# Two passages of a fused attention and two-layer expert kernel: where the order of experts is worked out, when a gather is issued, in how many parts rows are written

## The chip, the cores and the metric

The kernel runs on one core of one Trainium2 chip, as one program. The metric is the device time of an execution in microseconds (us). The core's engines work side by side, each through its own queue in order: PE (matmuls; PEld loads its weights), DVE, ACT, POOL, and SP, which here issues DMAs. Between engines semaphores order the work, so an instruction that waits holds back all that stands behind it on its engine.

## The reference

```python
def reference(**kwargs):
    ...
    attn_out = _attn_ref(**attn_kwargs)         # clustered attention: 2 x 8 heads x 768 x 64
    x = np.ascontiguousarray(attn_out.transpose(0, 2, 1, 3)).reshape(B * S, H * D)
    x = _moe_ref(x=x, **moe_kwargs)             # layer 1
    return _moe2_ref(x=x, **moe2_kwargs)        # layer 2

def _moe_ref(x, w_gate, w1, w2, capacity):      # 1536 tokens, 512 wide, 8 experts, 1024 inside
    ...
    expert_idx = np.argmax(logits, axis=1)      # one expert for each token
    ...
    h = np.maximum(np.einsum('ecd,edf->ecf', disp, w1), 0.0)
    y = np.einsum('ecf,efd->ecd', h, w2)
    ...
            out[i] = gate_w[i] * y[expert_idx[i], pos[i]]
```

Layer 2 is of the same kind, with a second gate (a sigmoid) and no capacity. Which tokens an expert gets is known only once the rows before it are done: layer 1 needs all of attention, layer 2 all of layer 1.

## The kernel before

Attention runs first, pair of heads by pair, and each half of a batch's rows is scaled and written to a table in DRAM, `x1d` (row: 512 values, gate, token number, one-hot). After that come eighteen **units**, nine of layer 1 (0 to 8) and nine of layer 2 (9 to 17). A unit is up to 392 rows of one expert. Experts are taken by size: the layer's largest first, in two units (128 and 64 rows in layer 1, 256 and 136 in layer 2), so that the first can start before all tokens are routed. Unit 7 has 168 rows, unit 8 (the last of layer 1) 120, unit 9 256, unit 10 136.

**A unit's work.** `gather` (POOL, an indirect DMA) fetches its rows, `meta` (POOL) reads their gate and token; `entry` turns 128 rows on PE and splits them into two float16 halves (`xh` on ACT, `xl` on DVE). `mm1` makes the inner values in eight steps f, of twelve matmuls each, into one of three PSUM buffers; ACT writes `hh`, and the rest `hl` comes either from DVE straight out of PSUM, or, for the f that `FP` lists for the unit, from ACT to `hr` and from there on POOL. `hr` has one buffer, so the next `hr` waits until POOL has read it. `mm2` makes the output in four steps d; in unit 9 it works by token (`pz`). `piece` splits half a weight tile as loaded (`raw`) into `wh` (ACT) and `wl` (DVE, one piece late); `PIECES` says before which f or d of a unit one is issued. A weight tile of 1 MB has four `raw` buffers; SP loads the next when a tile's second `wl` is done.

**Between the layers.** `run` goes through the units. Beside the matmuls it advances generators by one `yield` at set places (once before each step, in the first units of a layer where `SA` and `SB` say so); the engines' order is thus the order in which this code is written and its yields fall. `exit1` takes a unit of layer 1 out: it turns its rows back, works out their layer 2 logits (`pq`, `lt`, `lg`), and scales them; `routed` does the routing of a group of units: choice, place of each row in its expert's list, `R.codes` (low and high part of the place), write of the rows to the table `x2d`, `R.invert` (one-hots `av` and `rv` on DVE, whose matmul lists the rows of each expert by place), and `R.select`, which picks one expert's indices once `R.order` (eight to ten small DVE operations) has sorted the experts by count. The last group is units 6, 7 and 8. After group (4, 5), the "cut", layer 2's first two experts are fixed and unit 9's gather gets its indices (`idx2a`), from rows so far alone; after the last group unit 10 and those behind get theirs (`idx2`). Between attention and layer 1 `after_half` does the same with `x1d`: the last half batch is routed while unit 0 (128 rows) runs, and unit 1 is gathered when `idx1` is there.

Places the text speaks of: `after_half`'s `end` branch (L1560 to L1617), `hr` (L952 to L957), `run` (L1104 to L1121), `exit1`'s `rows` (L1688 to L1706), `routed` (L1796 to L1844).

Of the kernel before, what the change touches and what calls it, by code (L numbers as in the profile page):

```python
# [8 lines left out]
F32 = mybir.dt.float32  # L9
# [715 lines left out]
class MoE:  # L725
# [24 lines left out]
    FB = 0  # L750
    FP = {0: (2, 3, 4, 5, 6, 7), 5: (1, 3, 5), 7: (1, 3, 5, 7), 8: (1, 3, 5), 9: (3, 4)}
    FY = 7
    SA = (1, 1, 1, 0, 1, 0, 0, 0, 0, 0, 1, 1)
    SB = (1, 1, 1, 1, 1, 1, 1, 1, 1, 1, 1, 1)
    Q = 2

    def __init__(self, tc, ctx, ident, R, XW, ND, stages, ps_t):
        nc = tc.nc
        self.tc, self.nc, self.ident, self.R, self.XW, self.ND = tc, nc, ident, R, XW, ND
        DT = self.DT = F16  # L760
        self.pool = lambda name, bufs, **k: ctx.enter_context(tc.tile_pool(name=name, bufs=bufs, **k))
        self.ps_t = ps_t
        self.raw = self.pool("m_raw", 4, side="right")
        self.rings = []
        self.units = [u for s in stages for u in s.units]
        self.ranks = [(s, j) for s in stages for j in s.ranks]
        for s, r0 in zip(stages, (0, stages[0].E)):
            for u in s.units:
                u.r = r0 + s.ranks.index(u.j)
        self.most = max(u.rows for u in self.units)  # L770
        self.G = 4 * len(self.ranks)
        self.fl, self.flt, self.okr, self.reg = {}, {}, {}, {}
        self.rawt, self.chunk = {}, {}
        self.tasks, self.lows = [], []
        self.nload = self.nsplit = self.half = 0
        self.credit = 0
        self.ngather = self.nmeta = 0
        self.limit = self.RING - 1

# [155 lines left out]
    def mm1(self, u, f):  # L935
# [16 lines left out]
        if f in self.FP.get(self.units.index(u), ()):  # L952

            hr = self.sm.tile([128, 256], F32, tag="hr", name="hr", bufs=1)
            nc.scalar.activation(hr[:, :N], p[:, :N], AF.Relu)  # L955
            nc.gpsimd.tensor_tensor(hl[:, f, :N], hr[:, :N], hh[:, f, :N], op=ALU.subtract)
            return  # L957
# [117 lines left out]
    def run(self, task):  # L1075
# [3 lines left out]
        for i, u in enumerate(units):  # L1079
# [24 lines left out]
            for d in range(4):  # L1104
# [3 lines left out]
                if d == 3 and u.opens:  # L1108
                    self.need(4 * u.r + 3)
                    self.flags(u.r)  # L1110
                self.mm2(u, d)
                if d % 2 and u.closes:
# [5 lines left out]
            if head:  # L1118
                assert nxt.gt, "unit not gathered"
                for k in range(len(nxt.tiles)):  # L1120
                    self.entry(nxt, k)  # L1121
# [180 lines left out]
def tile_kernel(tc, q, k, v, centroids, wg1, w11, w12, cap_in, wg2, wog2, w21, w22, out,  # L1302
# [15 lines left out]
    with ExitStack() as ctx:  # L1318
# [27 lines left out]
        if True:  # L1346
# [87 lines left out]
            def after_half(b, hf, rows):  # L1434
# [125 lines left out]
                if end:  # L1560
# [5 lines left out]
                    pp = positions()  # L1566
                    turns(places(), gates(), load_order())
                    scale(2)
                    for i in (0, 2, 1):
                        write(nc.sync, slice(i, i + 1))  # L1570
# [17 lines left out]
                while not next(inv):  # L1588
                    if not end:
                        yield  # L1590
                yield
                if not end:
# [55 lines left out]
        def exit1(unit, ys):  # L1648
# [39 lines left out]
            def rows():  # L1688
# [7 lines left out]
                if group is groups[-1]:  # L1696
# [6 lines left out]
                    us = small("us", len(ns))  # L1703
                    nc.vector.scalar_tensor_tensor(us, u, XSUM, sx[:, ks], op0=ALU.mult, op1=ALU.mult)
                    for i, n in enumerate(ns):
                        nc.scalar.mul(xo[i][:n, :DM], ps[i][:n], us[:n, i:i + 1])  # L1706

            if unit is group[-1]:
# [4 lines left out]
        def routed(group, t0, T, rows):  # L1713
# [43 lines left out]
            if not last:  # L1757
                yield from turns_by(K[1], scales())
            for _ in range(1 if last else K[5]):
                yield  # L1760
# [35 lines left out]
            def gates():  # L1796
                yield from gate
                nc.vector.scalar_tensor_tensor(g2, rx, 1.0 / XSUM, g2, op0=ALU.mult, op1=ALU.mult)
                for i, (x, n) in enumerate(xos):
                    nc.gpsimd.tensor_copy(x[:n, DM:DM + 1], g2[:n, i:i + 1])  # L1800

            def write():
                r0 = 1 + group[0].row
                for x, n in xos:
                    nc.sync.dma_start(x2d[r0:r0 + n], x[:n])
                    r0 += n

            if last:
                turns(places(), load_order(), gates())
                write()  # L1810
# [4 lines left out]
            while not next(inv):  # L1815
                if not last and K[4]:
                    yield
            more = first_experts() if cut else iter(())
            for _ in range(KL if last else K[3]):
# [8 lines left out]
            if cut:  # L1828
                while next(more, more) is not more:
                    next(more, None)  # L1830
                    yield
                R.select(M.sm, ro[0], tab2, idx2a, 0, 1)
                s2.reg[:2] = [ro[1][0:1, j:j + 1] for j in range(2)]
                s2.units[0].src = x2d[:1 + group[-1].row + group[-1].rows]
                s2.units[0].idx = idx2a[:, 0]
            if last:
                RO = ro[0]
# [111 lines left out]
```

## Time and profile before

| | us |
|---|---|
| runs, median of 3 | 626.52 (625.83 to 628.45) |
| profiled execution | 623.46 |
| its span, first to last instruction | 621.7 |
| PE busy | 570.0 (92%) |
| DVE busy | 466.4 (75%) |
| ACT busy | 421.8 (68%) |
| POOL busy | 216.4 (35%) |

Times below are us from the start of the span. 1.8 us of the profiled execution lie outside the span. Busy shares are averages over all stages; a stage is read by the wait that ends last in it. An engine's idle time is put down to its releaser, the instruction whose end let it go on.

### The profile page before, as it was taken

The numbers are of one execution on the slowest core, as the hardware profiler recorded it, in microseconds if no ns is written. First come the engines' busy times: TensorE is split into PE (matmuls) and PEld (weight loads), VectorE is DVE, ScalarE is ACT, GpSimd is POOL, SyncE is SP. The second block draws the span as 40 slices with busy tenths as digits, with TensorE's granted clock in tenths as the row PEclk, the third lists the DMA queues.
The fourth block names the chain that finished last, engine by engine and source line by source line (L and its number), as shares of the span: only waits on it lengthen the run. The fifth ranks groups of instructions, "written<-read, shape, count | busy, mean of one in ns | idle before, by whom it ended". The sixth has DMA issues, their size and how long they took to land.

```text
span 621.7 us, 14524 instructions
## 1 busy us (share of the span) xinstructions
PE 570.0 (92%) x5428; PEld 467.1 (75%) x5428; DVE 466.4 (75%) x1185; ACT 421.8 (68%) x902; POOL 216.4 (35%) x427
## 2 busy tenths in 40 slices
PE   7899999998999998986799999997788999999993
PEld 2676767676767675656778998996777888999993
DVE  4776777677989676867577778789678566979881
ACT  3666666777676667963585687776774566979781
POOL 7702020201341110105743355636523723253541
PEclk9999999999999999999899999999999999999997
DMA  5589654656519891522456856976963677898930
GB/s 138 155 208 289 166 135 118 143 134 134 148 29 224 258 249 23 198 69 105 146 179 236 277 181 206 305 259 191 302 206 98 220 222 240 293 307 291 333 126 23
DMA packets 75518, 117.55 MB, mean 189 GB/s; under 512 B 10504, under 2 KB 43400, under 8 KB 75441
## 3 DMA queue, kind: packets, MB, share of 16 engines
q1 hardware_dynamic: 72017, 106.76, 57.4%
q0 software_dynamic: 3264, 9.72, 4.8%
q8 instruction: 45, 0.74, 0.5%
q14 instruction: 32, 0.26, 0.1%
q10 hardware_dynamic: 160, 0.07, 0.0%
HBM read 84.28 MB, written 12.87 MB: 156 GB/s over the span
## 4 chain that ended last, share of the span: by engine, by line
PE 61%; DVE 15%; ACT 11%; issue 4%; DMA 4%; POOL 2%; SPq 0%; ACTq 0%; DVEq 0%; POOLq 0%
PE ph L949 15%; PE py L1021 13%; PE av L280 9%; PE pss L238 8%; PE ppt L268 6%; PE pz L996 3%; DVE nm L246 3%; DVE wl L846 3%; ACT pe L254 2%; PE pyo L1637 2%; ACT wh L839 2%; ACT pt L270 1%; PE pxt L926 1%; PE plog L153 1%; DMA x2d<-xo 1%
## 5 line engine op out<-in xcount | busy, mean ns | idle before, releaser
L846 DVE SCALAR_TENSOR_TENSOR wl<-raw,sw,wh 128x1024 f16<-128x1024 f32 x128 | 163.6, 1285 | 19.0 <-ACT wh L839 18.8
L839 ACT ACTIVATE wh<-raw,sw 128x1024 f16<-128x1024 f32 x128 | 146.1, 1148 | 3.0 <-DMA x<-ot 2.5
L246 DVE TENSOR_REDUCE nm<-pss 128x1 f32<-128x768 f32 x96 | 91.4, 952 | 41.5 <-PE pss L238 37.8
L254 ACT ACTIVATE pe<-pss,nm 128x768 f32<-128x768 f32 x96 | 87.1, 907 | 24.3 <-DVE nm L246 24.3
L949 PEld LDWEIGHTS <-wh 128*128 128x128 f16 x1152 | 87.7, 99 | 17.4 <-issue 12.8
L238 PE MATMUL pss<-y,x 128*128 128x384 f32 x384 | 95.4, 370 | 4.0 <-ACT pe L254 3.2
L268 PE MATMUL ppt<-ident,pe 128*128 128x128 f32 x576 | 80.5, 275 | 3.3 <-ACT pt L270 1.4
L238 PEld LDWEIGHTS pss<-y,x 128*128 128x128 f32 x384 | 64.7, 194 | 24.6 <-issue 12.5
L270 ACT COPY pt<-ppt 128x384 f32<-128x384 f32 x128 | 57.9, 482 | 29.6 <-PE ppt L268 29.3
L949 PE MATMUL ph<-xh,wh 128*128 128x192 f16 (+14 forms) x576 | 67.3, 240 | 9.9 <-ACT hr L955 4.6
L268 PEld LDWEIGHTS ppt<-ident,pe 128*128 128x128 f32 x576 | 69.2, 142 | 8.9 <-ACT pt L270 2.3
L1021 PEld LDWEIGHTS <-wh 128*128 128x128 f16 x960 | 72.4, 99 | 4.3 <-issue 1.0
L280 PE MATMUL av<-pt,v 128*64 128x384 f32 x384 | 68.8, 494 | 0.0
L949 PE MATMUL ph<-xl,wh 128*128 128x192 f16 (+14 forms) x576 | 67.2, 240 | 0.4 <-DVE xl L928 0.3
L949 PE MATMUL ph<-xh,wl 128*128 128x192 f16 (+14 forms) x576 | 67.3, 240 | 0.0
L951 ACT ACTIVATE hh<-ph 128x128 f16<-128x128 f32 (+14 forms) x144 | 44.6, 316 | 25.9 <-PE ph L949 24.7
L958 DVE SCALAR_TENSOR_TENSOR hl<-ph,hh 128x192 f16<-128x192 f32 (+14 forms) x126 | 40.8, 335 | 26.1 <-ACT hh L951 25.9
L1021 PE MATMUL py<-hh,wh 128*128 128x192 f16 (+13 forms) x480 | 46.6, 239 | 1.5 <-ACT hh L951 1.0
L1021 PE MATMUL py<-hl,wh 128*128 128x192 f16 (+13 forms) x480 | 46.8, 239 | 0.5 <-DVE hl L958 0.2
L949 PEld LDWEIGHTS <-wl 128*128 128x128 f16 x576 | 45.5, 99 | 1.9
L280 PEld LDWEIGHTS av<-pt,v 128*64 128x64 f32 x384 | 24.8, 136 | 28.4 <-issue 28.3
L1021 PE MATMUL py<-hh,wl 128*128 128x192 f16 (+13 forms) x480 | 46.1, 239 | 0.0
(326 smaller groups left out, 873.4 us busy)
## 6 DMA issues: line engine op xcount, KB each, us to landing
raw<-in_moe_w SPq DMA_DIRECT2D x64, 1024.0 KB, 6.2
y<-kh SPq DMA_DIRECT2D x31, 192.0 KB, 4.0
x<-qh SPq DMA_DIRECT2D x30, 192.0 KB, 4.2
q<-in_q SPq DMA_DIRECT2D x8, 384.0 KB, 4.9
k<-in_k SPq DMA_DIRECT2D x8, 384.0 KB, 4.6
x<-ql SPq DMA_DIRECT2D x16, 192.0 KB, 3.5
v<-in_v SPq DMA_DIRECT2D x8, 384.0 KB, 3.3
out<-zt SPq DMA_DIRECT2D x1, 3072.0 KB, 11.3
```

Source lines behind the costliest of these rows:

```text
L238: nc.tensor.matmul(p[:, hf, :W], xx[:, c * P:(c + 1) * P], yy[:, hf * W:(hf + 1) * W], start=a, stop=o)
L246: nc.vector.tensor_reduce(nm, p[:, :, :W], axis=AX.XY, op=ALU.max, negate=True)
L254: nc.scalar.activation(pe, p[:, :, :W], AF.Exp, bias=d["nm", c, j], scale=1.0, accum_out=d["sm"][:, c, j:j + 1])
L268: nc.tensor.transpose(p[:, kc * P:(kc + 1) * P], pe[:, kh, kc * P:(kc + 1) * P], ident)
L270: eng(pt[:, kh * HALF:(kh + 1) * HALF, (c % HALF) * P:(c % HALF + 1) * P], p.rearrange("p (a b) -> p a b", a=HALF))
L280: nc.tensor.matmul(p[j * D:(j + 1) * D, :W], d["v"][:, j, kc, :], d["pt", hf, j][:, kc, :], start=(kc == 0), stop=(kc == C - 1))
L839: nc.scalar.activation(hi[:, :, s], x[:, :, s], AF.Copy, scale=sw)
L846: nc.vector.scalar_tensor_tensor(lo[:, :, s], x[:, :, s], sw, hi[:, :, s], op0=ALU.mult, op1=ALU.subtract, accum_out=fl)
L949: nc.tensor.matmul(p[:, :N], w[:, c, fs], x[:, c, :N], start=(k == 0), stop=(k == 11))
L951: nc.scalar.activation(hh[:, f, :N], p[:, :N], AF.Relu)
L958: nc.vector.scalar_tensor_tensor(hl[:, f, :N], p[:, :N], 0.0, hh[:, f, :N], op0=ALU.max, op1=ALU.subtract)
L1021: nc.tensor.matmul(p[:, :N], w[:, f, s], x[:, f, :N], start=(k == 0), stop=(k == 23))
```

## The change

Six edits:

1. `after_half`, `end`: the third row block is scaled (`scale(2)`) ahead of the places instead of after them, and the order of the experts (`load_order`) is worked out behind the inversion's one-hots instead of in turns with the places. `SA` gets a step before d = 1 of unit 0, so that the inversion's matmul stands on PE one d earlier.
2. `mm1`: `hr` is one tile kept for the whole run; units of at most 128 rows use its two halves in turns, by f.
3. `FP`: unit 7 has `hr` and POOL for f = 5, 7 instead of 1, 3, 5, 7; unit 8 for 1, 2, 5, 6 instead of 1, 3, 5.
4. `routed`, cut: indices are selected and the gather of unit 9 is issued as soon as the order is there, instead of after all of `first_experts`, and at once instead of at `run`'s next place for it.
5. `exit1`, `routed`, last group: the 512 values of the rows of units 6 and 7 are written to `x2d` when they are scaled, their last 12 columns (gate, token, one-hot) with unit 8's whole rows at the end, in reverse order of the units; the order of the experts behind the inversion's one-hots, as in 1; one `yield` more before the places, which puts f = 3 of unit 9 ahead of their matmuls on PE.
6. `PIECES` and `run`: a piece goes from d = 3 of unit 8 to f = 1 of unit 9, and unit 10's first 128 rows are turned before d = 3 of unit 9 instead of after it.

```diff
-              (0, 1, 0, 1, 1, 0, 0, 1, 1, 1, 1, 1),
-              (1, 0, 0, 0, 0, 0, 0, 0, 1, 1, 1, 1),
+              (0, 1, 0, 1, 1, 0, 0, 1, 1, 1, 1, 0),
+              (1, 1, 0, 0, 0, 0, 0, 0, 1, 1, 1, 1),
...
-    FP = {0: (2, 3, 4, 5, 6, 7), 5: (1, 3, 5), 7: (1, 3, 5, 7), 8: (1, 3, 5), 9: (3, 4)}
+    FP = {0: (2, 3, 4, 5, 6, 7), 5: (1, 3, 5), 7: (5, 7), 8: (1, 2, 5, 6), 9: (3, 4)}
     FY = 7
-    SA = (1, 1, 1, 0, 1, 0, 0, 0, 0, 0, 1, 1)
+    SA = (1, 1, 1, 0, 1, 0, 0, 0, 0, 1, 1, 1)
...
-            hr = self.sm.tile([128, 256], F32, tag="hr", name="hr", bufs=1)
+            if self.hr is None:
+                self.hr = self.sm.tile([128, 256], F32, tag="hr", name="hr", bufs=1)
+
+            hr = self.hr[:, f % 2 * 128:] if N <= 128 else self.hr
...
+                if d == 3 and head and prev:
+                    assert nxt.gt, "unit not gathered"
+                    self.entry(nxt, 0)
                 self.mm2(u, d)
...
-                for k in range(len(nxt.tiles)):
+                for k in range(1 if prev else 0, len(nxt.tiles)):
                     self.entry(nxt, k)
...
-                    turns(places(), gates(), load_order())
                     scale(2)
+                    turns(places(), gates())
...
+                if end:
+                    turns(load_order())
                 yield
...
                         nc.scalar.mul(xo[i][:n, :DM], ps[i][:n], us[:n, i:i + 1])
+                        if not unit.ends:
+                            nc.sync.dma_start(x2d[r0:r0 + n, :DM], xo[i][:n, :DM])
+                            r0 += n
...
-            for _ in range(1 if last else K[5]):
+            for _ in range(2 if last else K[5]):
...
-                turns(places(), load_order(), gates())
+                turns(places(), gates())
                 write()
...
+            if last:
+                turns(load_order())
...
             if cut:
-                while next(more, more) is not more:
-                    next(more, None)
-                    yield
+                while not ro:
+                    next(more)
                 R.select(M.sm, ro[0], tab2, idx2a, 0, 1)
...
+                if M.units[M.ngather] is s2.units[0]:
+                    M.gather()
+                while next(more, more) is not more:
+                    next(more, None)
+                    yield
```

DVE, attention to layer 1, from the order's last step to the first use of the listed rows, before (`p1RO`, `p1ordi`, `cnt`: the order; `av`, `rv`: the one-hots; `tab<-pinv`: the matmul's list):

```order
L636 TENSOR_TENSOR p1RO<-rank,iota 128x64
L640 TENSOR_TENSOR oe<-p1RO,iota 1x64
L644 TENSOR_REDUCE p1ordi<-oe 1x8
L1505 TENSOR_TENSOR cnt_3615<-cnt_3615,hs_97 128x8
L1474 TENSOR_SCALAR x<-x,sx 128x512
L1538 TENSOR_SCALAR pl<-code_81 128x6
L1542 TENSOR_TENSOR plf<-pl,hst_98 128x6
L1544 SCALAR_TENSOR_TENSOR vc<-plf,capc,val_82 128x6
L603 TENSOR_TENSOR av<-hi,blk 128x144
L604 TENSOR_TENSOR av<-av,vc 128x144
L611 TENSOR_TENSOR rv<-lo,iota 128x384 x2
L1603 TENSOR_TENSOR tab_127<-pinv,tab_127 128x24
```

and now:

```order
L611 TENSOR_TENSOR rv<-lo,iota 128x384 x2
L1504 TENSOR_TENSOR base_126<-base_126,ppos 128x8
L1507 TENSOR_TENSOR cnt_3615<-base_126,baseh 128x8
L1509 TENSOR_SCALAR cnt_3615<-cnt_3615,cap 128x8
L626 SCALAR_TENSOR_TENSOR key<-cnt_3615,rev_96 128x8
L629 TENSOR_TENSOR G<-key 128x64
L633 TENSOR_REDUCE rank<-G 128x8
L636 TENSOR_TENSOR p1RO<-rank,iota 128x64
L640 TENSOR_TENSOR oe<-p1RO,iota 1x64
L644 TENSOR_REDUCE p1ordi<-oe 1x8
L1512 TENSOR_TENSOR cnt_3615<-cnt_3615,hs_97 128x8
L1612 TENSOR_TENSOR tab_127<-pinv,tab_127 128x24
```

The ten operations of the order stand between the one-hots and `tab`, where nothing stood; the same ten are gone from the rows ahead of the one-hots.

POOL, unit 7, from its last `hl` to the gather of unit 9 (`xg<-x2d,idx2a`), before (`vbg`, `vbk`, `xo<-xg`, `tk`: exit of unit 6):

```order
L956 TENSOR_TENSOR hl<-hr,hh 128x168 x3
L1659 MEMSET lg 128x80
L1660 MEMSET am 128x5
L1681 COPY vbg<-vb 128x2
L1682 TENSOR_SCALAR vbk<-vb,okr 128x2
L1685 COPY xo<-xg 128x11
L1686 COPY tk_100<-xg 128x1
L1685 COPY xo<-xg 48x11
L1686 COPY tk_100<-xg 48x1
L886 DMA xg<-x2d,idx2a 128x524 x2
```

and now:

```order
L960 TENSOR_TENSOR hl<-hr,hh 128x168 x2
L1668 MEMSET lg 128x80
L1669 MEMSET am 128x5
L887 DMA xg<-x2d,idx2a 128x524 x2
L1690 COPY vbg<-vb 128x2
L1691 TENSOR_SCALAR vbk<-vb,okr 128x2
```

The two gathers went ahead of the exit's six small operations, which now stand behind their wait.

ACT, unit 8, f = 1 to 6, before:

```order
L951 ACTIVATE hh<-ph 128x120
L955 ACTIVATE hr<-ph 128x120
L951 ACTIVATE hh<-ph 128x120
L839 ACTIVATE wh<-raw,sw_108 128x4x256
L951 ACTIVATE hh<-ph 128x120
L955 ACTIVATE hr<-ph 128x120
L839 ACTIVATE wh<-raw,sw_108 128x4x256
L951 ACTIVATE hh<-ph 128x120
L927 CAST xh<-pxt 128x4x128
L951 ACTIVATE hh<-ph 128x120
L955 ACTIVATE hr<-ph 128x120
L927 CAST xh<-pxt 128x4x128
```

and now:

```order
L952 ACTIVATE hh<-ph 128x120
L959 ACTIVATE hr<-ph 128x120
L952 ACTIVATE hh<-ph 128x120
L959 ACTIVATE hr<-ph 128x120
L840 ACTIVATE wh<-raw,sw_108 128x4x256
L952 ACTIVATE hh<-ph 128x120
L840 ACTIVATE wh<-raw,sw_108 128x4x256
L952 ACTIVATE hh<-ph 128x120
L928 CAST xh<-pxt 128x4x128
L952 ACTIVATE hh<-ph 128x120
L959 ACTIVATE hr<-ph 128x120
L928 CAST xh<-pxt 128x4x128
```

The second `hr` comes from f = 2 instead of f = 3 and goes to the other half of the tile; between it and the third stand two `wh` pieces, two `hh` and an `xh`.

## Rows read from the trace of the kernel before

**Rows 1.** Windows of the span around the two passages: start:end, us, busy time by engine, PEclk.
```profile
285.00:299.53 14.53, 9.22 (x153) 8.47 (x153) 9.86 (x52) 4.08 (x17) 8.01 (x11) 1.00 0.32 109
299.53:310.00 10.47, 9.15 (x166) 8.07 (x167) 7.04 (x20) 7.25 (x18) 8.65 (x24) 0.84 0.48 168
310.00:418.00 108.00, 106.29 (x1179) 95.69 (x1175) 84.49 (x235) 80.56 (x153) 49.70 (x89) 1.00 0.73 239
418.00:440.00 22.00, 17.78 (x232) 16.66 (x230) 20.68 (x72) 15.56 (x35) 12.53 (x25) 1.00 0.62 199
440.00:459.00 19.00, 15.12 (x231) 13.42 (x229) 13.51 (x34) 14.21 (x32) 8.71 (x17) 1.00 0.78 259
488.50:600.00 111.50, 111.46 (x1331) 106.44 (x1329) 90.03 (x210) 85.60 (x160) 43.36 (x93) 1.00 0.82 268
```

**Rows 2.** Timeline, 286 to 300: start, us, engine, line, instruction, idle time and its releaser.
```profile
286.37 1.56 POOL L1476 TENSOR_SCALAR x<-x,sx 128x512 f32<-128x512 f32 x1 [0.86 <-ACT hh L951]
...
287.38 0.58 DVE L1502 TENSOR_SCALAR cnt<-cnt,cap 128x8 f32<-128x8 f32 x1
...
287.99 0.35 DVE L626 SCALAR_TENSOR_TENSOR key<-cnt,rev 128x8 f32<-128x8 f32 x1
...
289.64 0.14 DVE L1505 TENSOR_TENSOR cnt<-cnt,hs 128x8 f32<-128x8 f32 x1
...
289.71 0.47 DVE L1474 TENSOR_SCALAR x<-x,sx 128x512 f32<-128x512 f32 x1
...
291.54 1.25 DVE L611 TENSOR_TENSOR rv<-lo,iota 128x384 f16<-128x384 int32 x2
...
294.63 0.30 PE L616 MATMUL pinv<-av,rv 128*128 128x24 f16 x6
...
294.97 0.18 DVE L1603 TENSOR_TENSOR tab<-pinv,tab 128x24 f32<-128x24 f32 x1 [2.18 <-PE pinv L616]
...
295.87 1.04 POOL L886 DMA_INDIRECT xg<-x1d,idx  x1 [2.69 <-DVE w L662]
...
299.53 0.43 PE L926 MATMUL pxt<-ident,xg 64*128 64x64 f32 x4 [1.90 <-DMA xg<-x1d,idx]
```

**Rows 3.** Waits from 280 to 300: us in total, times, longest.
```profile
ACT hr L955 <- POOL hl L956: 3.8, 4, 2.0
```

**Rows 4.** Chain of waits from 405 to 500: start, us, what.
```profile
428.32 6.99 DMA x2d<-xo
...
438.42 5.73 DMA xg<-x2d,idx2a
...
475.84 10.49 PE pz L996 x96
```

**Rows 5.** Timeline, 434 to 453, columns as in Rows 2.
```profile
434.22 0.17 DVE L1826 TENSOR_TENSOR tab<-ppos,tab 128x32 f32<-128x32 f32 x1
...
437.94 0.19 DVE L665 TENSOR_REDUCE idx2a<-w 128x4 int32<-128x32 f32 x1
...
446.97 0.63 PE L926 MATMUL pxt<-ident,xg 128*128 128x128 f32 x4 [1.43 <-DMA xg<-x2d,idx2a]
...
447.89 0.27 ACT L955 ACTIVATE hr<-ph 128x120 f32<-128x120 f32 x1 [3.12 <-POOL hl L956]
...
452.07 0.21 PE L1021 MATMUL py<-hh,wh 128*128 128x120 f16 x1 [0.42 <-ACT hh L951]
```

**Rows 6.** DVE groups by shape from 420 to 440: count, busy us, mean ns.
```profile
L958 DVE SCALAR_TENSOR_TENSOR hl<-ph,hh 128x168 f16<-128x168 f32 x4 | 1.3, 323 | 0.0
```

**Rows 7.** Timeline, 469 to 489, columns as in Rows 2.
```profile
469.62 0.19 DVE L1771 TENSOR_TENSOR pos<-ppos,base 128x40 f32<-128x40 f32 x1
...
471.32 2.39 SPq L1805 DMA_DIRECT2D x2d<-xo  x5
...
472.89 1.36 DVE L611 TENSOR_TENSOR rv<-lo,iota 128x384 f16<-128x384 int32 x2
...
488.28 0.40 PE L949 MATMUL ph<-xl,wh 128*128 128x136 f16 x4 [0.34 <-DVE xl L928]
```

More of the change, by code (lines that the diff above doesn't have):

```diff
@@ L777, in __init__ @@
         self.ngather = self.nmeta = 0
+        self.hr = None
         self.limit = self.RING - 1
@@ L1704, in rows @@
                     nc.vector.scalar_tensor_tensor(us, u, XSUM, sx[:, ks], op0=ALU.mult, op1=ALU.mult)
+                    r0 = 1 + unit.row
                     for i, n in enumerate(ns):
                         nc.scalar.mul(xo[i][:n, :DM], ps[i][:n], us[:n, i:i + 1])
+                        if not unit.ends:
+                            nc.sync.dma_start(x2d[r0:r0 + n, :DM], xo[i][:n, :DM])
+                            r0 += n
             if unit is group[-1]:
@@ L1798, in gates @@
                 nc.vector.scalar_tensor_tensor(g2, rx, 1.0 / XSUM, g2, op0=ALU.mult, op1=ALU.mult)
-                for i, (x, n) in enumerate(xos):
+                for i, (x, n) in list(enumerate(xos))[::-1 if last else 1]:
                     nc.gpsimd.tensor_copy(x[:n, DM:DM + 1], g2[:n, i:i + 1])
@@ L1803, in write @@
                 r0 = 1 + group[0].row
-                for x, n in xos:
-                    nc.sync.dma_start(x2d[r0:r0 + n], x[:n])
+                todo = []
+                for i, (x, n) in enumerate(xos):
+                    c0 = DM if last and i < len(xos) - len(group[-1].tiles) else 0
+                    todo.append((x2d[r0:r0 + n, c0:], x[:n, c0:]))
                     r0 += n
+                for dst, x in todo[::-1 if last else 1]:
+                    nc.sync.dma_start(dst, x)
             if last:
-                turns(places(), load_order(), gates())
+                turns(places(), gates())
                 write()
```

## The prediction

> **What bounds the kernel now.** I read the windows first. PE is busy 106.29 of 108.00 us from 310 to 418 and 111.46 of 111.50 from 488.5 to 600 [rows 1]: there PE is the bound, so a shift that reaches 310 or 488.5 arrives whole at the end, and no other engine's saving counts there. The change touches what lies ahead of these two stretches, where PE is idle: 5.3 us of 14.53 up to 299.53, 4.2 of 22.00 from 418 to 440, 3.9 of 19.00 from 440 to 459 [rows 1]. Then, for each of these, I read the timeline for the wait that ends last, and the chain for what carries it.
>
> Passage 1 (attention to layer 1). PE waits 1.90 us for unit 1's rows at 299.53; the gather at 295.87 waited for its indices on DVE, and DVE had stood still 2.18 us until PE's `pinv` [rows 2]. DVE was done with `rv` at 291.54 + 1.25 = 292.79, but `pinv` came only at 294.63 [rows 2], behind two d of unit 0's mm2, which were late because ACT waited 3.8 us in four goes for POOL to read the single `hr` [rows 3].
>
> Passage 2 (layer 1 to layer 2). Unit 9's first gather is issued at 438.42, though the last of the rows it reads landed at 428.32 + 6.99 = 435.31 [rows 4] and the table was there at 434.22; what it waited for is `idx2a` at 437.94 [rows 5]. The late rows hold PE 1.43 us at 446.97, and ACT 3.12 us at 447.89: POOL's `hl` of unit 8 stands behind `meta`, which waits for the same rows. ACT is behind from there to the end of mm1, where PE waits for its last `hh` at 452.07 [rows 5].
>
> **The change part by part.** *Order behind the one-hots, passage 1.* Ten DVE operations leave the stretch ahead of `rv`. From `key` to the last `cnt` seven of them start in 289.64 − 287.99 = 1.65 us, 0.275 a step [rows 2]; with the one foreign operation among them taken off (0.15, as such rows last) and 0.3 for the three that ran in turns ahead of them (an estimate, 0.1 a step), about 1.9 us go, and `rv` ends at 290.9. Behind it the ten run alone, ten times 0.275 = 2.75, to 293.65. `tab` follows there if `pinv` is done, 1.0 sooner than now: it stands a d earlier and loses most of the 3.8 us of `hr` waits, so I count it as done. `tab` at 293.65 instead of 294.97 is 1.3 us; the gather, its landing and unit 1 move with it, and PE only waits longer ahead of them. Bounds: 2.2 (the whole idle time, if the order costs no more alone than in turns) and −0.3, by the next paragraph.
>
> `scale(2)` takes 0.47 us on DVE before and after the move [rows 2]; but it now comes when POOL begins its own scaling, 1.56 us from 286.37. During that one the 128x8 `cnt` took 0.58 and ended at 287.96, as POOL did at 287.93; the 128x8 `cnt` at 289.64 took 0.14 [rows 2]. So DVE does stand still beside POOL's scaling, for a part of it, and did so before as well; I add nothing, and keep 1.56 as the price if all of `scale(2)` waits: 1.3 − 1.56 = −0.3. The Trainium skill says in "SBUF — State Buffer", section "Who interferes with whom", that DVE and GpSimd share a port pair under an exclusive lock, which a tensor_scalar in a two-port mode takes, and that whoever comes second blocks fully. By that rule this sum is either 1.3 or about −0.3, depending on who is first; the rows show a stall of 0.4, not of 1.56.
>
> The writes of `x1d` move ahead with the gates and `scale(2)`, and were not what the gather waited for: nothing. The clock: PE's was 0.84 of 2.4 GHz on average from 299.53 to 310 after the 1.90 us of idle, that is at 1.2 GHz for about a third of it, which is worth 0.16 x 10.47 = 1.7 us of PE time [rows 1, 2]. The idle time before it grows now; I leave the loss as it is and keep −1.7 as a bound.
>
> *Gather of unit 9 at once.* The index operations follow `tab` directly (two of 0.19 at 434.22 and after: 434.6). Unit 7 gives two more `hl` to DVE, 2 x 0.323 = 0.65 [rows 6], on an engine busy 20.68 of 22.00 [rows 1]; with that the indices are there at 435.3, as the rows are. So the gather goes out at about 435.4, 3.0 earlier. Its tile for 446.97 is there at 444.0 and the 1.43 us are gone; POOL reads the first `hr` 3.0 sooner, so the wait that ended at 447.89 would end at 444.9, and ACT comes to it at 447.89 − 3.12 = 444.8. With two halves and f = 1, 2, 5, 6 the next `hr` that has to wait is later still. ACT then works through from 444.8 to the last `hh`: 3.12 saved, less one more `hr` of 0.27, less the 0.65 that unit 7's later DVE passes on to its end. **2.2 us.** Of the two new `hl` in unit 7 I expect no more: f = 6 of unit 7 waited for `hr`, now it waits for DVE's `hl` of f = 3, at about the same time. Bounds: 0, if ACT's saved wait is only moved (its window is busy 14.21 of 19.00 [rows 1]), and 3.12 + 1.43 = 4.5.
>
> What stands behind the gather on POOL are the exit's copies and `vbk`; they wait for the landing of the `x2d` rows with it, and nobody needs them before the last group's choice, thirty us later: nothing.
>
> *Rows in two parts.* Four writes of 512 columns now stand on SP ahead of weight loads, two and two, each some 2.39 / 5 = 0.48 [rows 7]: a load behind them is about 1.0 us late. With four `raw` buffers a load is issued three tiles ahead of its split, and no load is in the chain from 405 to 500: nothing, at most 1.9 if the cover is gone. At the end five writes remain, four of them of 48 bytes a row; they matter for unit 10's gather alone.
>
> *Order behind the one-hots, passage 2.* From `pos` at 469.62 to the end of `rv` at 472.89 + 1.36 = 474.25 are 4.63 us, with seven of the order's operations in turns [rows 7]; at 0.16 each, the width of such rows, 1.1 go, and `rv` ends at 473.15. Alone they take 7 x 0.275 = 1.9, to 475.05. The inversion's matmul no longer holds PE up ahead of f = 7, but DVE's `hl` of f = 5, whose PSUM buffer `pz` takes, now stands behind the order: 256 columns, about 0.4 by the 0.323 for 168 [rows 6], so 475.5 against 475.84 [rows 4]. **0.3 us**; between −0.8 (the order's extra time) and 1.1.
>
> *The piece moved and unit 10's first rows early.* The `wh` goes from ahead of `yt` to ahead of the second `hh` of unit 9, and `lg` waits on DVE behind that `hl`: nothing, and at most the time of that one `wh` both ways. Turning 128 rows before d = 3 costs PE the same, and hides the copy that PE waited for at 488.28 (0.34 [rows 7]); the eight rows that are left have a copy of their own: **0.2 us**, between −0.3 and 0.8.
>
> **The sum** is 1.3 + 2.2 + 0.3 + 0.2 = 4.0 us of the profiled execution's 623.46, of which 621.7 are the span. This execution ran 3.1 under the median of 626.52; I take the 4.0 off the median: 622.5.
>
> **Rivals.** *Unit 8 gains nothing* (15%): ACT's wait of 3.12 is filled by the pieces behind it, and PE gets its last `hh` when it did. For it: ACT splits five `wh` in this unit, over 14 busy us of 19. Against: they are the same five, and the wait was idle time. 1.8 left: 624.7.
>
> *DVE blocked by POOL in passage 1* (11%): `scale(2)` comes second and waits out POOL's scaling. For it: both become ready when `sx` is done. Against: the 0.58 of `cnt`. 4.0 − 1.56 = 2.4: 624.1. The rule of the Trainium skill named above is this rival's.
>
> *Unit 7 gains too* (10%): 4.2 us of PE idle time from 418 to 440 [rows 1] come from waits of which `hr` is the largest; if half of it goes, and the 0.65 isn't passed on, it is 4.0 + 2.1 + 0.65 = 6.8: 619.7. Against: DVE is full there.
>
> *PE waits for unit 10's rows* (12%, slower): the transposes now stand on PE ahead of the last quarter of `pz`, so a gather that is late stops PE, where before it had 10.49 us of `pz` [rows 4] to hide in. The quarter starts at 475.5 + 7.9 = 483.4; the last small write is issued at about 471.32 + 2.39 − 1.1 = 472.6 [rows 7], and a gather lands in 5.73 [rows 4]. So the writes have 483.4 − 5.73 − 472.6 = 5.1 us to land. With the 6.99 seen at 428.32 [rows 4] PE would lose 1.9. It is slower in all when they take over 5.1 + 4.0; slower by over 0.5% from 5.1 + 4.0 + 3.1 = 12.2 on: 629.7. Against: those 6.99 were whole rows, beside weight loads; these are 48 bytes a row.
>
> **Chances.** What is left, 52%, is the forecast, whose own range is 620.0 to 624.5. About 0.5%, 3.1 us, is what a measurement here can tell from no change. Faster by more: 0.46 of the forecast's 0.52, 0.03 of the blocked case's 0.11, all of unit 7's 0.10: 0.59. Slower by more: 0.12. The rest 0.29. The range for 8 in 10 takes in unit 7's case, unit 8's and the clock's bound: 618.8 to 626.6.
>
> **What would show it.** Right: `pinv` done and DVE without idle time between `rv` and `tab`, the gather of unit 1 at 294.6 or so; the gather of unit 9 within a us of the landing of the rows it reads, no wait of ACT for POOL over 1 us in unit 8, PE's last wait there 2 to 3 us sooner; DVE's order right behind `rv` in unit 9, and PE in `pz` held by `hl`. Wrong: `scale(2)` longer than a us; a raw load as releaser of a `wh`; PE waiting for `xg<-x2d,idx` inside `pz`; PE idle anew behind 310 or 490.

## The result and the profile after

The changed kernel took 618.26 us (median of 4 runs, 615.39 to 620.57), the kernel before 626.17 beside it: ratio 0.9892, interval 0.9846 to 0.9939. Repeated with 10 and 30 runs it was 615.47 against 622.46, with a ratio of 0.9918, 0.9885 to 0.9952: about 5 us faster, 3.0 to 7.2 by the interval. (The ratio is not that of the two medians, which lie 7.0 us apart.) The forecast was 4.0 faster, 622.5 within 618.8 to 626.6, counted from 626.52; from there the two ratios make 619.8 and 621.4, while the 618.26 itself lies 0.5 below the range. The ratios leave out a kernel's slowest executions where they fell out of line, such as one of 1122.35 us in (5).

The attention, which the change doesn't touch, ends at another time in each execution, so I count from the start of its last `avo` copy (279.58 before, 275.19 after) to the start of PE's `pxt` of unit 1, of the `ppos` at the start of unit 7 (128x32), of the `us` at the end of unit 7, of that at the end of unit 8 and of the first `pz`, and to the end of the span. (The `us` that closes a unit's stretch belongs to the exit of the unit before it, which runs there.) A star marks a stretch with a mean granted clock of 0.83 to 0.92; all others of units 7 to 9 and of the first column have 1.00. Layer 1 begins with 10.5 us at a mean clock of 1.00 in (2), (3) and (4), of 0.67 in (5), and of 0.84 in all the others. The numbers in brackets are those of the experiments below.

| kernel | to unit 1 | layer 1 | unit 7 | unit 8 | unit 9 | from `pz` | sum |
|---|---|---|---|---|---|---|---|
| before | 19.95 | 120.66 | 19.11 | 19.32 | 17.06 | 146.02 | 342.12 |
| before again (1) | 19.47 | 120.78 | 19.16* | 20.48* | 17.06 | 145.96 | 342.91 |
| after | 18.13 | 120.80 | 20.69* | 15.86 | 16.82 | 146.01 | 338.31 |
| after again (2) | 18.02 | 120.17 | 19.08 | 16.45 | 16.81 | 144.95 | 335.48 |
| passage 1 alone (3) | 17.94 | 120.17 | 19.12 | 19.58 | 17.05 | 145.96 | 339.82 |
| passage 1 put back, hr kept (4) | 17.64 | 120.20 | 19.08 | 16.19 | 16.82 | 144.94 | 334.87 |
| one hr (5) | 18.48* | 124.12 | 20.69* | 17.81 | 16.82 | 145.99 | 343.91 |
| gather late (6) | 18.48* | 121.48 | 19.02 | 23.49* | 16.80 | 146.07 | 345.34 |
| old list of f (7) | 18.01 | 121.51 | 19.26* | 18.17 | 16.81 | 145.95 | 339.71 |
| gather alone (9) | 19.68 | 120.80 | 19.23* | 18.85* | 17.06 | 145.97 | 341.59 |
| rows whole (10) | 17.98 | 120.77 | 20.69* | 15.85 | 16.79 | 145.48 | 337.56 |
| hr and list, no early gather (12) | 18.17 | 121.20 | 19.02 | 16.99 | 17.05 | 146.31 | 338.74 |
| okr late, order behind `hl` (8) | 17.72 | 121.05 | 18.34 | 16.48 | 14.93 | 146.97 | 335.49 |
| and `ls` early (11) | 17.71 | 120.43 | 18.31 | 16.49 | 14.93 | 145.36 | 333.23 |

Timeline of the changed kernel in passage 1, for [rows 2]: start, us, engine, line, instruction, idle time and releaser.
```profile
281.95 0.46 DVE L1481 TENSOR_SCALAR x<-x,sx 128x512 f32<-128x512 f32 x1
281.99 1.85 POOL L1483 TENSOR_SCALAR x<-x,sx 128x512 f32<-128x512 f32 x1 [0.86 <-DVE pre L1468]
...
285.66 1.48 DVE L611 TENSOR_TENSOR rv<-lo,iota 128x384 f16<-128x384 int32 x2
...
286.84 0.60 PE L616 MATMUL pinv<-av,rv 128*128 128x24 f16 x6
...
289.08 0.14 DVE L1512 TENSOR_TENSOR cnt<-cnt,hs 128x8 f32<-128x8 f32 x1
289.15 0.16 DVE L1612 TENSOR_TENSOR tab<-pinv,tab 128x24 f32<-128x24 f32 x1
...
290.03 1.04 POOL L887 DMA_INDIRECT xg<-x1d,idx  x1 [3.30 <-DVE w L662]
...
293.32 0.43 PE L927 MATMUL pxt<-ident,xg 64*128 64x64 f32 x4 [1.85 <-DMA xg<-x1d,idx]
```
DVE no longer stands still ahead of `tab`; `pinv` was done 1.7 us before. ACT's waits for POOL, 3.8 us in four goes [rows 3], are one:
```profile
ACT hr L959 <- POOL hl L960: 1.3, 1, 1.3
```
Units 7, 8 and 9 of the changed kernel, windows with columns as in [rows 1]:
```profile
414.12:434.81 20.69, 16.54 (x193) 15.27 (x191) 18.03 (x64) 12.52 (x28) 11.21 (x21) 0.92 0.75 238
434.81:450.67 15.86, 14.76 (x236) 13.68 (x235) 13.60 (x33) 14.52 (x33) 9.24 (x16) 1.00 0.90 289
450.67:467.49 16.82, 13.31 (x125) 10.75 (x122) 12.81 (x58) 9.90 (x24) 3.71 (x10) 1.00 0.44 140
```
In unit 8 PE is idle 1.1 us; it was 3.9 in a window of 19.00 [rows 1]. Its timeline, for [rows 5]:
```profile
426.81 0.14 DVE L1044 TENSOR_SCALAR okr<-pq 128x1 f32<-128x1 f32 x1
...
426.98 0.31 ACT L1678 COPY lt<-pq 128x176 f32<-128x176 f32 x1 [3.76 <-DVE okr L1044]
...
427.34 0.59 PE L1683 MATMUL pq<-sel,lt 128*128 128x16 f32 x4 [1.77 <-ACT lt L1678]
...
428.51 0.19 DVE L665 TENSOR_REDUCE idx2a<-w 128x4 int32<-128x32 f32 x1
...
429.62 1.61 POOL L887 DMA_INDIRECT xg<-x2d,idx2a  x1 [4.96 <-DVE rev L651]
...
444.46 0.21 PE L1025 MATMUL py<-hh,wh 128*128 128x120 f16 x1 [0.34 <-ACT hh L952]
```
The gather follows its indices by 1.1 us, `pxt` and `hr` of unit 8 wait for nothing long, and the last `hh` holds PE as shortly as before (in the repetition `hr` waits 0.52 and the last `hh` holds PE 0.99). Unit 9 and the start of unit 10, for [rows 7]:
```profile
465.49 0.15 DVE L1791 TENSOR_TENSOR cnt<-ppos,hs 128x8 f32<-128x8 f32 x1
...
467.03 1.06 DVE L962 SCALAR_TENSOR_TENSOR hl<-ph,hh 128x256 f16<-128x256 f32 x3
...
467.49 1.03 PE L1000 MATMUL pz<-wh,hh 128*128 128x256 f16 x8 [1.52 <-DVE hl L962]
...
475.34 0.60 PE L927 MATMUL pxt<-ident,xg 128*128 128x128 f32 x4
...
479.29 0.40 PE L950 MATMUL ph<-xh,wh 128*128 128x136 f16 x4 [0.38 <-ACT xh L928]
479.53 0.40 PE L950 MATMUL ph<-xl,wh 128*128 128x136 f16 x4
```
The order stands behind `rv`, `pz` waits for the `hl` behind it, and unit 10's rows are there when PE turns them.

### The profile page after: what moved, and what is told of

It reads as the page before. It is cut to its first block, busy times and chain, and to the rows that moved or that the text cites. A ratio compares the mean times of both kernels' runs of the same rounds, so it can differ in the third digit from the quotient of the medians.

```text
span 613.5 us, 14527 instructions
## 1 busy us (share of the span) xinstructions
PE 565.1 (92%) x5428; PEld 466.1 (76%) x5428; DVE 466.1 (76%) x1186; ACT 421.3 (69%) x901; POOL 215.4 (35%) x426
## 4 chain that ended last, share of the span: by engine, by line
PE 61%; DVE 17%; ACT 12%; issue 4%; DMA 3%; SPq 1%; ACTq 0%; POOL 0%; DVEq 0%
PE ph L950 15%; PE py L1025 13%; PE av L280 9%; PE pss L238 7%; PE ppt L268 6%; PE pz L1000 3%; DVE nm L246 3%; DVE wl L847 3%; ACT wh L840 3%; ACT pe L254 2%; PE pyo L1646 2%; PE pxt L927 2%; ACT pt L270 1%; ACT xo L1700 1%; DVE hl L962 1%
## 5 line engine op out<-in xcount | busy, mean ns | idle before, releaser
L238 PE MATMUL pss<-y,x 128*128 128x384 f32 x384 | 93.6, 365 | 4.8 <-ACT pe L254 3.2
L238 PEld LDWEIGHTS pss<-y,x 128*128 128x128 f32 x384 | 63.2, 190 | 25.2 <-issue 13.2
```

The costliest lines, as they stand in the source:

```text
L238: nc.tensor.matmul(p[:, hf, :W], xx[:, c * P:(c + 1) * P], yy[:, hf * W:(hf + 1) * W], start=a, stop=o)
```

## The experiments

**1 and 2. Both kernels again.**

> The kernel before, unchanged. In its first profile the last copy of the attention (the last row of avo) started 279.58 us into a span of 621.7, so 342.1 us lay behind it; in the changed kernel it was 275.19 and 338.3. Theory: the 4.4 us ahead of that copy are drawn anew in every execution, in code that the change doesn't touch; then the 342.1 comes back within 0.6 and the 279.58 does not, and the ratio of times is 1.00. Rival: the change shortens the attention too; then both numbers come back.

> The changed kernel, unchanged. Theory: 338.3 us behind the last avo copy come back within 0.6, the time ahead of it lies anywhere from 275 to 280, and the ratio of times settles near 0.9935 (4.0 us). Rival (the attention is shortened too): 275.2 comes back, ratio 0.987 to 0.989. Second question: TensorE's clock in unit 7 (0.92 granted on average from 418 to 440, 1.00 before) is low again if PE's idle time of 1.8 us ahead of pyo is what lowers it.

Before again: ratio 1.0017 (0.9990 to 1.0044), last `avo` copy at 274.29. After again: 278.02. So the 4.4 us ahead of that copy were chance: in all kernels it lay between 274.3 and 280.2. What lies behind it came back within 0.8 for the kernel before, but not for the changed one, 335.48 instead of 338.31; 0.6 had been allowed. Four stretches differ: in layer 1 (0.6 shorter in the repetition) and unit 7 (1.6 shorter) the clock does too; unit 8 is 0.6 longer, so that units 7 and 8 together gain 1.0 only; and 1.06 lie behind `pz`, all of it behind the issue of the last output (9.06 us to the end, then 7.77). In unit 7 PE had the same 1.77 us of idle time ahead of the `sel` matmuls both times. Windows behind them, of the changed kernel first:
```profile
428.00:430.00 2.00, 2.00 (x15) 1.82 (x15) 1.90 (x9) 0.98 (x3) 0.38 (x1) 0.61 0.53 66
430.00:432.00 2.00, 2.00 (x18) 2.00 (x16) 1.88 (x7) 0.70 (x1) 1.70 (x2) 0.54 1.04 398
```
and of its repetition:
```profile
429.00:431.00 2.00, 1.57 (x14) 1.48 (x15) 1.90 (x9) 1.35 (x2) 0.00 (x0) 1.00 0.52 194
431.00:433.00 2.00, 2.00 (x31) 2.00 (x29) 2.00 (x8) 1.53 (x3) 1.20 (x1) 1.00 0.83 228
```
The first ran largely at 1.2 GHz (18 matmuls in its second window), the repetition at 2.4 (31). So this idle time doesn't decide on the clock by itself. In (1), (7) and (9) unit 7 had a low clock ahead of the same wait instead of behind it, and the wait took most of it up. The wait in the kernel before, then in (1):
```profile
433.48 0.59 PE L1674 MATMUL pq<-sel,lt 128*128 128x16 f32 x4 [1.48 <-ACT lt L1669]
```
```profile
427.89 0.59 PE L1674 MATMUL pq<-sel,lt 128*128 128x16 f32 x4 [0.46 <-ACT lt L1669]
```
Unit 7 took 0.05 to 0.15 longer there. In these traces a low clock is dear behind a wait and cheap ahead of one.

**3 and 4. Each passage alone.** In 4 `hr` keeps its halves:
```diff
-    SA = (1, 1, 1, 0, 1, 0, 0, 0, 0, 1, 1, 1)
+    SA = (1, 1, 1, 0, 1, 0, 0, 0, 0, 0, 1, 1)
...
+                    turns(places(), gates(), load_order())
                     scale(2)
-                    turns(places(), gates())
...
-                if end:
-                    turns(load_order())
```


> The kernel before with the edits of the passage from attention to layer 1 alone (scale(2) ahead, order behind the one-hots, SA, hr in two halves for units of up to 128 rows). Theory: what the two traces show from the last avo copy to the end of that passage, 1.7 us, reaches the end: 340.4 us behind the copy, ratio 0.997. Rival: part of it is lost again in layer 1 or is due to the second passage's edits: 341 to 342.

> The changed kernel with the first passage put back as it was (order in turns with places, scale(2) behind, SA), hr in two halves kept. Theory: the second passage gives 2.1 us (unit 7 loses 1.6, units 8 to 10 gain 3.7): 340.0 behind the last avo copy, ratio 0.9965. Rival: unit 7's loss hangs on the first passage's timing; then 338.5 to 339.

Passage 1 alone: 339.82, ratio 0.9970 (0.9943 to 0.9997), as the theory had it, though 0.5 of it lies in layer 1, at the higher clock. With the passage put back and `hr` kept: 334.87, ratio 0.9922 (0.9896 to 0.9949): less than both the theory's 340.0 and the rival's 338.5, and not slower than the whole change. The gather of unit 1 came 14.45 behind the `avo` copy, sooner than the 14.82 of the changed kernel (16.29 before):
```profile
ACT hr L959 <- POOL hl L960: 1.1, 1, 1.1
```
is ACT's wait for POOL there. So the two halves of `hr` alone carry the first passage; the order behind the one-hots, `scale(2)` ahead and the step in `SA`, which (4) puts back together, take 0.37 back.

**5. One `hr`.**
```diff
-            if self.hr is None:
-                self.hr = self.sm.tile([128, 256], F32, tag="hr", name="hr", bufs=1)
-
-            hr = self.hr[:, f % 2 * 128:] if N <= 128 else self.hr
+            hr = self.sm.tile([128, 256], F32, tag="hr", name="hr", bufs=1)
```


> The changed kernel with one hr of full width again, everything else kept. Theory A (hr in turns carries the first passage): ACT waits for POOL again, the two d ahead of pinv are late again, pinv comes at 15.0 us behind the last avo copy as before (11.65 changed) and the gather of unit 1 at about 16 (14.8 changed, 16.3 before). Theory B (the order behind the one-hots and scale(2) ahead carry it): 14.8 stays. In unit 8, where f = 1 and 2 follow each other into one hr, the stretch between the two us of units 7 and 8 (16.2 to 16.5 undisturbed) grows by 0.3 to 1.0.

Ratio 0.9977 (0.9942 to 1.0012). Between the theories: ACT waits again (waits of passage 1, and the timeline of `tab`),
```profile
ACT hr L956 <- POOL hl L957: 3.7, 4, 2.3
```
```profile
291.82 0.18 DVE L1609 TENSOR_TENSOR tab<-pinv,tab 128x24 f32<-128x24 f32 x1 [0.36 <-PE pinv L616]
```
but the order now fills DVE's wait for `pinv`, which stands a d earlier: the gather came at 15.33, 0.96 sooner than before. The clock fell ahead of `pinv` there:
```profile
287.39:289.39 2.00, 1.89 (x22) 1.76 (x20) 1.93 (x6) 0.93 (x5) 1.21 (x2) 0.61 0.56 208
289.39:291.39 2.00, 1.98 (x21) 1.81 (x20) 1.76 (x9) 0.72 (x3) 0.92 (x2) 0.53 0.52 195
```
Up to the 0.36 of `tab`'s wait may be due to that; without it the gather would come at 14.97 at the soonest (an estimate), near theory B. (6), with the halves and a low clock in the same place, had 15.20. So the two edits reach the same idle time from two sides: alone 0.96 (at most 1.32 by that estimate) and 1.84, together 1.47. Layer 1 took 3.5 longer than before, with a wait of 2.6 for `xh` in unit 1 and a clock of 0.67 behind it; what of it is due to `hr` is not shown. Unit 8 took 1.95 longer than in the first trace of the changed kernel, whose unit 7 had the same low clock; 0.3 to 1.0 had been expected.

**6. The gather in its old place.**
```diff
-                while not ro:
-                    next(more)
+                while next(more, more) is not more:
+                    next(more, None)
+                    yield
                 R.select(M.sm, ro[0], tab2, idx2a, 0, 1)
...
-                if M.units[M.ngather] is s2.units[0]:
-                    M.gather()
-                while next(more, more) is not more:
-                    next(more, None)
-                    yield
```

> The changed kernel with unit 9's indices and gather back behind the rest of the index work, in their old places. Theory A (the gather at once carries unit 8): the stretch between the us of units 7 and 8 goes from 16.2 to 16.5 back to 19.0 to 19.6, ACT's wait for POOL of 3 us is back. Theory B (hr in turns and the new list of f on POOL carry it): 16.2 to 17.2.

Ratio 1.0003 (0.9965 to 1.0041): all is lost, but by a third way, since unit 8 takes 23.49, more than either theory has. SP's queue and its longest wait, and ACT's timeline behind it:
```profile
SPq L1718 <- ACT xo L1716: 11.5, 2, 11.3
```
```profile
437.58 0.89 SPq L1718 DMA_DIRECT2D x2d<-xo  x2
439.66 1.03 SPq L811 DMA_DIRECT2D raw<-in_moe_w  x2
```
```profile
447.15 1.15 ACT L840 ACTIVATE wh<-raw,sw 128x1024 f16<-128x1024 f32 x1 [6.18 <-DMA raw<-in_moe_w]
```
With the indices, the code fixes the first experts later too, and these loads follow that in SP's queue. The experts were sorted on DVE by 430.20, but the loads now stand behind the early row writes, which wait for ACT's `xo`; in the changed kernel they stand ahead of them (427.82 and 435.85). So it doesn't tell A from B; 9 and 12 do.

**7. The old list of f on POOL.**
```diff
-    FP = {0: (2, 3, 4, 5, 6, 7), 5: (1, 3, 5), 7: (5, 7), 8: (1, 2, 5, 6), 9: (3, 4)}
+    FP = {0: (2, 3, 4, 5, 6, 7), 5: (1, 3, 5), 7: (1, 3, 5, 7), 8: (1, 3, 5), 9: (3, 4)}
```


> The changed kernel with the list of f on POOL as before (unit 7: 1, 3, 5, 7; unit 8: 1, 3, 5). As forecast (unit 7 passes on 0.65 for two more hl on DVE): unit 7, from its ppos to its us, 19.08 in the changed kernel, falls by 0.65, and unit 8 stays within 0.4 of 16.3. Rival: unit 7 is held by what follows mm1 (lt waits for okr, which stands behind wl on DVE) and stays within 0.2; rival for unit 8: the new list is half of its gain, 17.5 or more.

Ratio 0.9929 (0.9907 to 0.9951). Unit 8 18.17: the rival, since in this list all three f are odd and all go to one half. Unit 7 19.26 with a low clock: the 0.65 doesn't show in it, nor in the undisturbed 19.11 and 19.08 of before and after.

**9 and 12. The gather alone, and the halves with the new list alone.** 9 is the kernel before with the lines that 6 takes out put in; 12 is 3 with the list of the changed kernel.

> The kernel before, with only the indices and the gather of unit 9 put right behind the table (one hr, the old list of f, nothing else changed). As forecast, the gather carries the whole 3.12 us of ACT's wait for POOL in unit 8: the stretch from unit 7's us to unit 8's falls from 19.3 to 16.3 to 17. Rival, after the run with the old list of f (18.2 there, where all three f of unit 8 go to the same half of hr): the gather alone gives about 1, ACT still waits 2 for POOL, 18.0 to 18.5; the rest needs two halves in turns. The first passage stays at 16.3 to its gather.

> The kernel before with the edits of the first passage (hr in two halves among them) and the new list of f on POOL, but unit 9's indices and gather in their old places and the rows written whole. Theory (the halves with the new list carry unit 8, since the next hr that has to wait is that of f = 5 instead of f = 3): units 7 and 8 together, 38.4 to 38.7 in the kernel before and 35.3 to 35.5 in the changed one, undisturbed by the clock, come to 36.5 to 37.3. Rival (only together with the early gather, since PE and POOL wait for the rows of the gather all the same): 38.2 or more. The first passage repeats 14.8 to its gather.

The gather alone: ratio 0.9996 (0.9970 to 1.0021), unit 8 18.85, only 0.5 shorter, with a low clock in it: half of what the rival had. POOL and ACT there:
```profile
433.29 1.11 POOL L886 DMA_INDIRECT xg<-x2d,idx2a  x1 [5.02 <-DVE wl L846]
...
440.84 1.18 POOL L907 TENSOR_SCALAR vb<-xg 128x1 f32<-128x1 f32 x1 [3.02 <-DMA xg<-x2d,idx2a]
...
443.90 0.41 POOL L956 TENSOR_TENSOR hl<-hr,hh 128x120 f16<-128x120 f32 x1
...
444.34 0.27 ACT L955 ACTIVATE hr<-ph 128x120 f32<-128x120 f32 x1 [2.73 <-POOL hl L956]
```
The `hl` still stands behind `meta`: 3.02 of wait, then four operations to 443.90. From the first gather's issue to its landing, windows before and in (9):
```profile
438.42:444.15 5.73, 5.24 (x87) 4.96 (x84) 4.35 (x14) 5.73 (x12) 3.17 (x4) 1.00 0.88 311
```
```profile
433.29:440.69 7.40, 6.91 (x110) 6.68 (x108) 5.63 (x19) 7.01 (x17) 4.21 (x10) 1.00 1.01 364
```
Counted from the `us` that ends unit 7 (439.30 and 436.22), the gather is issued 2.05 sooner, but its rows land only 0.38 sooner: the way takes 7.40 instead of 5.73, with the DMA engines' mean busy share at 1.01 instead of 0.88. The second of two 1 MB weight loads was issued 2.43 ahead of the gather before, and beside it here (433.26). All traces with the landing on record agree: 5.28 to 5.73 with the late gather (before, 1, 3), 6.84 to 8.05 with the early one (2, 4, 9, 10, 11). That the loads are the cause was not tried apart. The halves with the list alone: ratio 0.9919 (0.9884 to 0.9954), units 7 and 8 36.01 together, a little under the theory's 36.5 to 37.3:
```profile
440.00 0.28 ACT L959 ACTIVATE hr<-ph 128x120 f32<-128x120 f32 x1
440.30 0.28 ACT L959 ACTIVATE hr<-ph 128x120 f32<-128x120 f32 x1
...
444.17 1.21 POOL L960 TENSOR_TENSOR hl<-hr,hh 128x120 f16<-128x120 f32 x3
...
444.61 0.27 ACT L959 ACTIVATE hr<-ph 128x120 f32<-128x120 f32 x1 [1.01 <-POOL hl L960]
```
POOL is as late, but ACT needs it only at f = 5. Of the 2.9 us of units 7 and 8 (38.43 before, 35.53 in (2)) the halves with the list bring 2.4 and the gather 0.5, one trace each.

**10. Rows written whole.**
```diff
-                        if not unit.ends:
-                            nc.sync.dma_start(x2d[r0:r0 + n, :DM], xo[i][:n, :DM])
-                            r0 += n
...
-                c0 = DM if last and i < len(xos) - len(group[-1].tiles) else 0
+                c0 = 0
```


> The changed kernel with the rows of units 7 and 8 written whole at the end, as before (no early writes of their 512 columns). Forecast: the two parts give nothing by themselves; everything stays within 0.3, also the stretch from pz to the end (145.0 to 146.0). Rival: five whole writes land later, unit 10's gather waits for them on POOL (it was issued 1.4 us behind the start of pz) and PE stops at its rows inside pz, for 1 to 3 us.

Ratio 0.9954 (0.9924 to 0.9983). Unit 10's gather goes out 0.9 later and PE still doesn't wait; the stretches repeat those of the first trace of the changed kernel, low clock in unit 7 included, and 145.48 from `pz` lies between its two values. As forecast, nothing.

**8 and 11. A version built on the runs.** Both start from (4). In (8) `okr` goes behind the matmuls with `sel`, and the order of passage 2 behind one more `hl`:
```diff
-            M.rank_ok(unit, pq[:, 511 - 2 * E * len(ns):])
             lt = M.sm.tile([P, max(prof1)], F32, tag="e1lt", name="lt", bufs=1)
             nc.scalar.copy(lt[:, :N], pq[:, :N])
...
+            M.rank_ok(unit, pq[:, 511 - 2 * E * len(ns):])
             xo = [M.xo.tile([P, XW], F32, tag="xo", name="xo") for _ in ns]
...
-            if last:
-                turns(load_order())
...
-            for _ in range(KL if last else K[3]):
+            for i in range(KL if last else K[3]):
                 yield
+                if last and i == 1:
+                    turns(load_order())
```
In (11) `ls` and its memset, moved from `outs` into `sums`, also come at f = 0 of `mm1`:
```diff
+            if u.by_token:
+                self.sums(u)
```


> The changed kernel with the first passage's order and scale(2) put back, hr in turns kept; in exit1 the matmul and the DVE operation of okr stand behind lt and the matmuls with sel; and in the second passage the order stands on DVE behind one more hl (f = 5 of unit 9). Theory: unit 7 loses PE's wait of 1.8 ahead of pyo, 19.08 to 17.5; pz no longer waits for DVE, us of unit 8 to pz 16.8 to 15.4; 332 behind the last avo copy, ratio about 0.987. Rivals: DVE is full in unit 7 (18 us of 19), so the wait turns up again in front of the next hl: 18.7 or more; and pz that begins 1.4 earlier waits for unit 10's rows instead, which come no sooner: 146 from pz to the end instead of 145.

> The kernel of the run before (okr behind lt, order behind one more hl, first passage's order as it was), and the memset of the column ls of the units by token moved to the start of their mm1. There DVE wrote ls only behind the wl of a weight piece, 5.3 us after pz began, and ACT could copy no pz before that; it came late to unit 10's xh, and PE waited 1.41 for it. Theory: the first copy of pz comes 2.5 us sooner, PE's wait for xh falls to 0.4, pz to the end 147.0 to 146.0 or less: 334.0 or less behind the last avo copy, ratio about 0.985. Rival: xh stands behind a wh on ACT anyway and PE waits over 1 us as before.

(8): ratio 0.9863 (0.9829 to 0.9898). Against (4) unit 9 is 1.9 shorter, PE's wait of 1.52 ahead of `pz` among it, and unit 7 0.74; but from `pz` on it is 2.0 longer, half of it at the start of unit 10, half behind the last output's issue, and layer 1 is 0.85 longer at a lower clock. The sum is 335.49, where 332 was expected:
```profile
471.52 0.07 DVE L968 MEMSET ls<- 128x8 f32 x1
471.69 0.47 ACT L1002 ACTIVATE xo<-pz,u 128x256 f32<-128x256 f32 x1 [4.44 <-PE pz L1000]
...
478.96 0.40 PE L950 MATMUL ph<-xh,wh 128*128 128x136 f16 x4 [1.41 <-ACT xh L928]
```
The wait is put down to PE, whose first `pz` ended long before: the copy starts as `ls` is written. With `ls` early, in (11):
```profile
470.86 0.47 ACT L1008 ACTIVATE xo<-pz,u 128x256 f32<-128x256 f32 x1 [1.70 <-PE pz L1006]
...
479.85 0.40 PE L952 MATMUL ph<-xh,wh 128*128 128x136 f16 x4 [0.39 <-ACT xh L928]
```
PE waits 0.39, as expected; 333.23 in all, ratio 0.9859 (0.9815 to 0.9903). By the ratios both are about 8.5 us faster than the kernel before. That they are faster than the changed kernel, whose interval overlaps, is not shown: beside (2) the sums give 2.3 for (11) and nothing for (8).

## Why the prediction was right, and where it wasn't

The direction and the size came out, but both large terms of the sum were credited to the wrong edit.

**Order behind the one-hots, passage 1: 1.3 forecast, 1.47 measured, mostly by another cause.** `rv` and `tab` stand without idle time between them, as forecast. But the 1.3 was the order's, and the halves of `hr` came into it only so far that `pinv` "stands a d earlier and loses most of the 3.8 us of `hr` waits". The halves alone give 1.84 (4), and the order with its companions takes 0.37 of that back; with one `hr` they are worth 0.96 (5). Alone behind `rv` the order took 2.0 us (285.66 + 1.48 to 289.15) where 2.75 was counted. That the number fits is luck in part.

`scale(2)` did not wait: 0.46. POOL's operation beside it, which came second, took 1.85 instead of 1.56 [rows 2]; it is 1.84 or 1.85 in all eight traces with this order and 1.56 in the six others. By the rule of the Trainium skill cited in the prediction ("SBUF — State Buffer", "Who interferes with whom") whoever comes second blocks: the trace agrees as far as it was POOL that got longer, by 0.29 of the 0.42 that DVE's operation still had to run.

**The clock.** It was left "as it is", rightly as a mean and wrongly as a fixed loss: unit 1 ran at 0.84 in both traces of before, and once each way in the changed kernel, worth 0.6 where 1.7 was kept as a bound. That it could fall behind the wait in unit 7, worth 1.0 over units 7 and 8, was not foreseen; of the seven traces with the new list and that wait it did in three (after, 5, 10) and not in 2, 4, 6 and 12.

**Gather of unit 9 at once: 2.2 forecast, 2.9 measured in (2) and 1.9 in the first trace, by another cause.** This is the step that failed: "Its tile for 446.97 is there at 444.0", so that "POOL reads the first `hr` 3.0 sooner, so the wait that ended at 447.89 would end at 444.9". An early gather was given the landing time of the late one. In (9) it went out 2.05 sooner and took 7.40 us instead of 5.73, so POOL began `meta` 0.38 sooner and read the first `hr` 0.47 sooner, and ACT still waited 2.73 instead of 3.12. What brings the gain are `hr` in halves and the list 1, 2, 5, 6: they move the first `hr` that has to wait from f = 3 to f = 5. The prediction had named this ("later still") without counting it. The rival *unit 8 gains nothing* would have been nearly right for the gather by itself. The 0.65 for unit 7 didn't come: 19.11 and 19.08.

**Rows in two parts: 0, and 0 in (10).** The price if the cover is gone, "at most 1.9", was too small: in (6) ACT waited 6.18.

**Order behind the one-hots, passage 2: 0.3 forecast, 0.24 measured**, with PE held by `hl` as forecast; the order was not tried apart from the `yield` and the piece that move with it. (8) shows what the place cost: one `hl` further on PE's 1.52 are gone.

**Unit 10's rows early: 0.2 forecast.** From the start of `pz` to its second four matmuls 12.60 before (475.68 to 488.28), 12.04 after: 0.56. It is still there at PE's last instruction in (2), (4), (10) and (11), about 136.9 behind the start of `pz` instead of 137.46, and lost by then in the first trace, (6) and (7) (137.4 to 137.6). The slower rival did not come: PE did not wait for unit 10's rows inside `pz` in any run.

**The sum**: 1.5 + 2.9 + 0.24 + 0.56 = 5.2 us, 0.8% of 622, against the forecast's 4.0 and the measured ratio of 0.9918. It takes (2), the trace with the higher clocks; with units 7 and 8 of the first trace it is 4.2.

## What to carry to other kernels

When a shared buffer makes one engine wait for another, count how long an earlier transfer will take in its new place, and what stands ahead of the reader on its own engine, before crediting it: here two halves in turns, with a list that uses them, were worth five times the early gather (2.4 and 0.5 us). Two edits that remove the same idle time don't add up, so try each without the other. Count from a point that the change can't touch, and take two traces of each kernel, before naming a stretch a loss. When a writer is moved earlier in a queue, look which loads now stand behind it and what they wait for.

## What the runs showed of the hardware

The same program, with the same idle time of PE, ran the stretch behind it once at a granted clock of 0.54 to 0.61 and once at 1.00 (2); where the low clock came ahead of a wait of 1.48 us, the wait shrank to 0.39 to 0.46 and the unit took 0.05 to 0.15 longer. The same gather landed in 5.28 to 5.73 us behind weight loads issued some 2.4 us before it, and in 6.84 to 8.05 beside them. POOL's 128x512 scaling took 1.56 us, and 1.84 or 1.85 when DVE's own had begun 0.04 us before it. The part from the start to the end of the attention varied between 274.3 and 280.2 us, with its first `nm` at 14.7 to 18.4, about as much as the whole gain.
